# Retention plus mixture of adapters on one core: the last unit finished batch by batch, and x turned back earlier in two rounds

## The chip, the cores and the metric

The kernel runs on one core of a Trainium2 chip. The metric is the device time of one execution in microseconds. Three executions of the kernel before took 198.21, 193.67 and 198.88 us, median 198.21 us. One more execution was recorded by the profiler; it took 192.59 us.

## The reference, cut to what matters

Eight batches of eight heads, 576 positions of width 64, go through a retention (attention without softmax, with a decay for each head). Its output x, 4608 tokens of width 512, then goes through eight low-rank adapters of rank 16, of which each token uses the best two.

```python
scores = scale * q @ k.T                       # each batch and head, 576 x 576
x = (scores * Dmat) @ v                        # Dmat = gamma[h] ** (i - j) for i >= j, else 0
logits = x @ w_gate                            # 4608 x 8
w = softmax over the two largest logits
out = x + sum over those two e of w_e * (x @ A[e]) @ B[e]
```

## The kernel before, in words

**Units.** The work is cut into 18 units. Units 0 to 15 are 128 positions of a pair of batches (four chunks of positions, four pairs). Units 16 and 17 are what is left of the 576 positions: 64 positions of four batches each. Such a unit holds, on its 128 partitions, the 64 positions of one batch on the lower half and of another batch on the upper half, twice side by side; index `t` names the half and index `b` the side. Its result leaves in four stores of 64 rows (128 KB each, line 513), that of a full unit in two stores of 128 rows (256 KB each, line 508).

**Stages of a unit.** Each is a function that issues its instructions on fixed engines:

- `stage_T`/`evict_T` (`turn`): transposes k and then q on TensorE into PSUM tiles `pt_k` (banks x0, x1) and `pt_q` (banks s0, s1); ScalarE copies them out as `kT`, `qT` (lines 215, 202, 240, 235).
- `stage_U`, `stage_A`, `put_state` (`sums`, `put`): the products of k and v that carry the state from chunk to chunk (`pu`, line 300). Only full units have them; units 16 and 17 have none.
- `stage_S`, `masks` (`scores`): the scores in `ps_s` (line 269), then four masked copies by VectorE (line 289).
- `stage_X`, `evict_x` (`products`): x, transposed, in `px` (banks x0, x1, line 350); ScalarE copies it out as `xT` (line 366, for units 16 and 17 line 371).
- `stage_Z`, `routing_1` (`logits`): the products with A and w_gate in `pz` (bank x0, line 393), copied out by ScalarE as `zs` (line 406).
- `routing_2` (`choose`): VectorE finds the largest two logits (`m`, `ns`, `ge`, lines 416 to 421). `routing_3`: ScalarE's sigmoid `sg` (line 431). `routing_4`: GpSimd makes the weights `cm` (line 441) and the weighted `zc` (line 443).
- `stage_P`, `evict_z` (`small`): TensorE transposes `zc` into `pzt` (bank x1, line 378), ScalarE copies it out as `zT` (line 386).
- `stage_B` (`back`): TensorE turns x back into `po` (banks o0, o1, line 459). `stage_Y`, `evict_o` (`output`): it adds the products with B on top (line 475), and ScalarE copies the sums out as `osb`, two copies, one for each half `ho` (line 490). `store`: SyncE's queue issues the stores.

**Order.** It is written out by hand; each engine runs its instructions in the order in which the program issues them. The first rounds are listed singly. From round t = 5 on, a loop (line 726) works on several units at once: scores of unit t, logits of t - 1, `small`, `back` and `output` of t - 2, and `turn` of t + 1. Rounds 15 and 16 turn units 16 and 17, which have no state products, so no `sums` stand between `small` and `turn`. Round 17 does scores and products of the last unit, round 18 its logits and choice, round 19 what is left of it. The stores of unit t - 3 are issued at the head of round t, and those of unit 17 at the very end. All stores and nearly all loads go through SyncE's queue; one load (`Bcat`, line 588) goes through GpSimd's.

Of the kernel before, what the change touches and what calls it, by code (L numbers as in the profile page):

```python
# [10 lines left out]
FP32 = mybir.dt.float32  # L11
FP16 = mybir.dt.float16

ALU = mybir.AluOpType
AFT = mybir.ActivationFunctionType
# [3 lines left out]
def kernel(  # L19
# [10 lines left out]
    nc = tc.nc  # L30
    B, H, S, Dh = q.shape
    Ntok, Dm = out.shape
    E = moe_w_gate.shape[1]
    R = moe_A.shape[2]
    ER = E * R
    HP = H // 2
# [9 lines left out]
    scale = 1.0 / float(np.sqrt(Dh))  # L46
# [16 lines left out]
    for c in range(NFULL):  # L63
# [17 lines left out]
    mo = ctx.enter_context(tc.tile_pool(name="moe", bufs=2))  # L81
    pp = ctx.enter_context(tc.tile_pool(name="pp", bufs=1, space=bass.MemoryType.PSUM))
# [6 lines left out]
    ident16 = cpool.tile([128, 128], FP16, tag="ident16", name="ident16", align_bytes=256)  # L89
    warm = cpool.tile([128, 1], FP32, tag="warm", name="warm")  # L90
    zero = cpool.tile([128, 512], FP16, tag="zero", name="zero")
    AW = cpool.tile([128, HP, ER + E], FP32, tag="AW", name="AW", align_bytes=256)
    Bcat = cpool.tile([128, Dm], FP16, tag="Bcat", name="Bcat", align_bytes=256)
    id64 = pack[:, 0:64]
# [9 lines left out]
    units = [(c, bp) for c in range(NFULL) for bp in range(NP)] + [  # L104
        (NFULL, qd) for qd in range(NQ)
    ]
    NU = len(units)
    st = {u: {} for u in range(NU)}
# [6 lines left out]
    def is_full(u):  # L115
        return u < NU and units[u][0] < NFULL
# [18 lines left out]
    def load(u, w):  # L135
        if u >= NU:
            return
        c, bp = units[u]
        s0 = 128 * c
        if c == NFULL:  # L140
            for t in range(2):
                hf = slice(64 * t, 64 * t + 64)
                dst = block(u, t)[hf] if w == "v" else nt(u, w)[hf]
                nc.sync.dma_start(out=dst, in_=rows(w, 4 * bp + 2 * t, 2, s0, 64))
        elif w == "v":
            for t in range(2):
                hf = slice(64 * t, 64 * t + 64)
                nc.sync.dma_start(  # L148
                    out=block(u, t)[hf], in_=rows(w, 2 * bp, 2, s0 + 64 * t, 64)
                )  # L150
        elif w == "q" and paired(u):
            for b in range(2):
                nc.sync.dma_start(  # L153
                    out=nt(u, w)[64 * b : 64 * b + 64].rearrange("p (h e) d -> p h (e d)", e=2),
                    in_=q[2 * bp + b, :, s0 : s0 + 128, :].rearrange(
                        "h (p e) d -> p h (e d)", e=2
                    ),
                )
        else:
            nc.sync.dma_start(out=nt(u, w), in_=rows(w, 2 * bp, 2, s0, 128))  # L160
# [118 lines left out]
    def masks(u, b=None, order=((0, 0), (1, 0), (0, 1), (1, 1))):  # L279
        for t, ho in order:  # L280
            hf = slice(64 * t, 64 * t + 64)
            out, in0 = facing(u, t, ho)[hf], st[u]["ps"][ho][hf]
            m = (trp if paired(u) else tri)[hf].unsqueeze(1)
            if b is None:
                m = m.unsqueeze(1).broadcast_to((64, 2, HP, ST))
            else:
                out, in0 = out[:, b], in0[:, b]
                m = m.broadcast_to((64, HP, ST))
            nc.vector.tensor_tensor(out=out, in0=in0, in1=m, op=ALU.mult)  # L289
# [28 lines left out]
    def first_state(u):  # L318

        c, bp = units[u]  # L320
        if c == NFULL:
            for t in range(2):
                put_state(u, t, SP[2 * bp + t], nc.gpsimd)
        elif c > 0:
            put_state(u, 0, SP[bp], nc.gpsimd)
# [77 lines left out]
    def routing_1(u):  # L403
        s = st[u]
        zs = mo.tile([128, 2, ER + E], FP32, tag="zs", name="zs")
        nc.scalar.copy(out=zs, in_=s["pz"])  # L406
        s["zs"] = zs
# [19 lines left out]
    def routing_3(u):  # L427
        s = st[u]
        sg = mo.tile([128, 2, E], FP32, tag="sg", name="sg")
        for b in range(2):  # L430
            nc.scalar.activation(  # L431
                out=sg[:, b, :], in_=s["zs"][:, b, ER : ER + E], func=AFT.Sigmoid,
                bias=s["ns"][:, b : b + 1], scale=2.0,
            )
        s["sg"] = sg

    def routing_4(u):
        s = st[u]
        cm = mo.tile([128, 2, E], FP32, tag="cm", name="cm")
        zc = mo.tile([128, 2, ER], FP16, tag="zc", name="zc")  # L440
        nc.gpsimd.tensor_tensor(out=cm, in0=s["ge"], in1=s["sg"], op=ALU.mult)  # L441
        for b in range(2):
            nc.gpsimd.tensor_tensor(
                out=zc[:, b, :].rearrange("p (e r) -> p e r", e=E),
                in0=s["zs"][:, b, 0:ER].rearrange("p (e r) -> p e r", e=E),
                in1=cm[:, b, :].unsqueeze(2).broadcast_to((128, E, R)),
                op=ALU.mult,
            )
        s["zc"] = zc
# [20 lines left out]
    def stage_Y(u):  # L470
        s = st[u]
        bv = Bcat.rearrange("p (a o d) -> p a o d", a=HP, o=2)
        for ho in range(2):
            for b in range(2):
                nc.tensor.matmul(  # L475
                    s["po"][ho][:, b, :, :],
                    lhsT=s["zT"][:, b, :],
                    rhs=bv[:, :, ho, :],
                    start=False,
                    stop=True,  # L480
                    skip_group_check=True,
                )

    def evict_o(u):
        s = st[u]
        s["osb"] = mo.tile(
            [128, 2, HP, 2, 64], FP32, tag="osb", name="osb", bufs=3, align_bytes=256
        )
        for ho in range(2):
            nc.scalar.copy(out=s["osb"][:, :, :, ho, :], in_=s["po"][ho])  # L490

    def fill(n):
        if n == 0:
# [7 lines left out]
    o3 = out.rearrange("(b s) m -> b s m", s=S)  # L501

    def store(u):
        c, bp = units[u]
        of = st.pop(u)["osb"].rearrange("p b a o d -> p b (a o d)")
        for b in range(2):
            if c < NFULL:
                nc.sync.dma_start(
                    out=o3[2 * bp + b, 128 * c : 128 * c + 128, :], in_=of[:, b]
                )  # L510
            else:
                for t in range(2):
                    nc.sync.dma_start(
                        out=o3[4 * bp + 2 * t + b, 128 * c : 128 * c + 64, :],
                        in_=of[64 * t : 64 * t + 64, b],
                    )
# [21 lines left out]
    for dt in range(HP):  # L538
        nc.sync.dma_start(  # L539
            out=AW[:, dt, 0:ER].rearrange("p (e r) -> p e r", e=E),  # L540
            in_=moe_A[:, 128 * dt : 128 * dt + 128, :].rearrange("e d r -> d e r"),
        )
    nc.sync.dma_start(
        out=AW[:, :, ER : ER + E],
        in_=moe_w_gate.rearrange("(t p) e -> p t e", p=128),
# [9 lines left out]
    def has(u):  # L555
        return 0 <= u < NU
# [3 lines left out]
    for r in range(2):  # L560
        sl = slice(64 * r, 64 * r + 64)
# [53 lines left out]
    def ahead(t):  # L615
        for u in {4: (0,), 5: (1, 2)}.get(t, (t - 3,)):
            if t > 3 and has(u):
                store(u)
        for w in "kqv":
            load(t + 4, w)  # L620
        if has(t + 1):
            first_state(t + 1)
        if has(t + 2):
            scale_(t + 2, "k", pool2)
            scale_(t + 2, "q", pool2)

    def scores(u):
        if has(u):
            stage_S(u)
            masks(u)  # L630

    def turn(u):
        if has(u):
            for w in "kq":
                stage_T(u, w)
                evict_T(u, w)

    def back(u):
        if has(u):
            stage_B(u)  # L640

    def logits(u, tag="x0"):
        if has(u):
            stage_Z(u, tag)
            routing_1(u)

    def small(u, tag="x1"):
        if has(u):
            stage_P(u, tag)
            evict_z(u)  # L650

    def choose(u):
        if has(u):
            routing_2(u)
# [12 lines left out]
    def products(u):  # L667
        if has(u):
            stage_X(u)
            evict_x(u)  # L670

    def output(u):
        if has(u):
            stage_Y(u)
            evict_o(u)

    ahead(2)
    stage_A(2)
    logits(0)
# [43 lines left out]
    back(2)  # L723
    output(2)

    for t in range(5, NU + 2):
        if has(t - 2):
            routing_4(t - 2)
        ahead(t)
        scores(t)  # L730
        logits(t - 1)
        small(t - 2)
        choose(t - 1)
        sums(t + 1)
        if has(t - 1):
            routing_3(t - 1)
        turn(t + 1)
        back(t - 2)
        put(t + 1)
        if has(t + 1):  # L740
            shift_q(t + 1, nc.vector)
        products(t)
        output(t - 2)
    store(NU - 1)
    return


# [28 lines left out]
```

## Time and profile before

| what | before |
|---|---|
| three executions | 198.21, 193.67, 198.88 us |
| the profiled execution | 192.59 us |
| its span | 190.8 us |
| TensorE busy | 168.5 us, 88% of the span |
| ScalarE, VectorE, GpSimd busy | 114.5, 111.7, 109.2 us |
| mean granted clock of TensorE | 0.98 |

The span runs from the first to the last recorded instruction; the profiled execution's own time is 1.8 us longer. Times of rows are microseconds from the start of the span. PE is TensorE, PEld its weight loads, DVE is VectorE, ACT is ScalarE, POOL is GpSimd, SPq is SyncE's queue of DMA issues; a q behind an engine's name means its sequencer. fp32 matmuls show as two records each.

### The profile page before, as it was taken

What the parts mean: (1) busy time and instruction counts of PE and PEld (TensorE: products, weight loads), DVE (VectorE), ACT (ScalarE), POOL (GpSimd) and SP (SyncE); (2) the same over time, 40 slices, a digit from 0 to 9 for tenths busy, and PEclk for the clock granted to TensorE, in tenths of its full rate; (3) what the DMA queues carried; (4) which work ended last, traced back from release to release, by engine and by line L of the source; (5) the groups of instructions that cost most, each with busy time, mean ns of one, the idle gap of its engine ahead of it and who ended that gap; (6) DMA issues with size and microseconds to landing.
All of it is one profiled execution on the core that took longest, in us unless ns stands there. A gap on an engine that the chain in (4) does not pass through costs nothing.

```text
span 190.8 us, 10293 instructions
## 1 busy us (share of the span) xinstructions
PE 168.5 (88%) x4607; PEld 147.7 (77%) x4607; DVE 111.7 (59%) x220; ACT 114.5 (60%) x254; POOL 109.2 (57%) x161
## 2 busy tenths in 40 slices
PE   7879799858999799989999999999988999999940
PEld 2566588756888699979998898999977898889920
DVE  1593768345078286858778776768675745646000
ACT  3537081802855939576786849395867586584660
POOL 1336206459619979593958768586959396420220
PEclk9999999998799999999999999999999999999995
DMA  6999999989999999999989999999996902303245
GB/s 144 256 265 231 182 151 232 228 176 243 253 200 246 267 273 264 251 246 267 243 206 269 248 240 261 274 243 262 226 244 155 246 12 107 113 4 113 82 121 131
DMA packets 108139, 38.99 MB, mean 204 GB/s; under 512 B 88768, under 2 KB 103488, under 8 KB 108096
## 3 DMA queue, kind: packets, MB, share of 16 engines
q1 hardware_dynamic: 107952, 38.21, 81.5%
q8 instruction: 36, 0.59, 1.3%
q0 software_dynamic: 144, 0.13, 0.4%
q14 instruction: 7, 0.06, 0.1%
HBM read 29.02 MB, written 9.44 MB: 202 GB/s over the span
## 4 chain that ended last, share of the span: by engine, by line
PE 64%; SPq 17%; ACT 4%; issue 3%; DVE 3%; DMA 3%; POOL 1%; ACTq 0%; POOLq 0%; DVEq 0%
PE pz L393 16%; PE px L350 16%; PE ps_s L269 8%; PE pu L300 6%; PE pt_k L215 5%; PE po L475 5%; PE po L459 5%; SPq L153 4%; SPq L148 4%; DMA q<-in_q_dram 3%; SPq L160 3%; SPq L539 3%; PE pt_q L202 3%; SPq L521 1%; PE pzt L378 1%
## 5 line engine op out<-in xcount | busy, mean ns | idle before, releaser
L350 PE MATMUL px<-qT,v 128*64 128x64 f32 (+1 forms) x576 | 39.5, 226 | 3.5 <-issue 2.5
L179 POOL TENSOR_TENSOR k<-k,pack 128x512 f32<-128x512 f32 x32 | 35.1, 1115 | 13.1 <-DMA k<-in_k_dram 12.1
L350 PE MATMUL px<-x,v 128*64 128x64 f32 (+1 forms) x576 | 40.0, 225 | 1.2 <-issue 0.5
L350 PEld LDWEIGHTS px<-x,v 128*64 128x64 f32 (+1 forms) x576 | 36.4, 139 | 4.6 <-issue 2.0
L289 DVE TENSOR_TENSOR x<-ps_s,pack 64x512 f32<-64x512 f32 (+1 forms) x38 | 25.1, 660 | 24.1 <-PE ps_s L269 23.8
L350 PEld LDWEIGHTS px<-qT,v 128*64 128x64 f32 (+1 forms) x576 | 35.9, 139 | 3.0 <-issue 1.6
L393 PE MATMUL pz<-AW,xT 128*128 128x136 f32 x288 | 38.1, 285 | 0.1
L393 PEld LDWEIGHTS pz<-AW,xT 128*128 128x128 f32 x288 | 34.5, 190 | 2.0 <-ACT osb L490 0.7
L169 POOL TENSOR_TENSOR qs<-q,pack 128x512 f32<-128x512 f32 x27 | 27.5, 1038 | 5.5 <-DMA q<-in_q_dram 5.4
L441 POOL TENSOR_TENSOR cm<-ge,sg 128x16 f32<-128x16 f32 x18 | 4.2, 231 | 42.9 <-ACT sg L431 20.4
L406 ACT COPY zs<-pz 128x272 f32<-128x272 f32 x18 | 6.9, 386 | 35.1 <-PE pz L393 35.1
L269 PE MATMUL ps_s<-qT,kT 64*64 64x64 f32 x1152 | 23.2, 222 | 4.2 <-issue 3.5
L269 PEld LDWEIGHTS ps_s<-qT,kT 64*64 64x64 f32 x1152 | 19.7, 134 | 7.8 <-issue 5.2
L289 DVE TENSOR_TENSOR qT<-ps_s,pack 64x512 f32<-64x512 f32 (+1 forms) x38 | 25.1, 660 | 1.1
L316 POOL COPY v<-SP 64x512 f32<-64x512 f32 x32 | 20.0, 625 | 1.6
L253 DVE COPY x<-qT 64x512 f32<-64x512 f32 x17 | 15.9, 933 | 7.5 <-ACT qT L235 4.3
L490 ACT COPY osb<-po 128x512 f32<-128x512 f32 x36 | 19.2, 587 | 0.7 <-PE po L475 0.6
L366 ACT COPY xT<-px 128x512 f32<-128x512 f32 x28 | 16.4, 624 | 4.8 <-PE px L350 4.8
L300 PE MATMUL pu<-v,k 64*64 64x64 f32 x1024 | 19.2, 221 | 0.1
L240 ACT COPY kT<-pt_k 128x512 f32<-128x512 f32 x34 | 18.2, 585 | 0.9 <-PE pt_k L215 0.7
L300 PEld LDWEIGHTS pu<-v,k 64*64 64x64 f32 x1024 | 16.9, 134 | 1.7 <-DVE SP L335 0.3
L252 DVE COPY x<-qT 64x512 f32<-64x512 f32 x14 | 8.5, 607 | 15.4 <-ACT qT L235 11.4
(46 smaller groups left out, 232.4 us busy)
## 6 DMA issues: line engine op xcount, KB each, us to landing
v<-in_v_dram SPq DMA_DIRECT2D x36, 256.0 KB, 4.9
q<-in_q_dram SPq DMA_DIRECT2D x34, 256.0 KB, 5.4
out_dram<-osb SPq DMA_DIRECT2D x32, 256.0 KB, 4.3
k<-in_k_dram SPq DMA_DIRECT2D x15, 512.0 KB, 5.6
k<-in_k_dram SPq DMA_DIRECT2D x6, 256.0 KB, 4.8
out_dram<-osb SPq DMA_DIRECT2D x8, 128.0 KB, 2.4
q<-in_q_dram SPq DMA_DIRECT2D x1, 512.0 KB, 7.7
AW<-in_moe_A_dram SPq DMA_DIRECT2D x4, 64.0 KB, 3.8
```

The source lines that it names most:

```text
L169: engines[b].tensor_tensor(out=qs[:, :, 4 * b : 4 * b + 4, :].rearrange("p e h d -> p h e d"), in0=tl[:, b * H : b * H + H, :].rearrange(" ...
L179: engines[b].tensor_tensor(out=tl[:, b * H : b * H + H, :], in0=tl[:, b * H : b * H + H, :], in1=g[:, c, :].unsqueeze(2).broadcast_to((128 ...
L240: nc.scalar.copy(out=tl[:, r], in_=st[u]["p" + w][r])
L253: eng.tensor_copy(out=x2[0:64, 1, b], in_=qT[64:128, 1, b])
L269: nc.tensor.matmul(ps[ho][64 * t : 64 * t + 64, b, hp, :], lhsT=kT[sl, t, b, hp, :], rhs=qT[sl, t, b, hp, :], start=(hp == 0 and b == bs[0 ...
L289: nc.vector.tensor_tensor(out=out, in0=in0, in1=m, op=ALU.mult)
L300: nc.tensor.matmul(pu[t][64 * ho : 64 * ho + 64, b, hp, :], lhsT=kn[sl, h, :], rhs=block(u, t)[sl, h, :], start=(hp == 0 and b == 0), stop ...
L316: copy(out=dst[:, :, :, ho, :], in_=src[64 * ho : 64 * ho + 64])
L350: nc.tensor.matmul(px[b][64 * ho : 64 * ho + 64, hp, t, :], lhsT=block(u, t)[rw, b * H + 2 * hp + ho, :], rhs=facing(u, t, ho)[rw, b, hp, ...
L366: nc.scalar.copy(out=xt.rearrange("p a (t i e) -> p (a t) e i", t=2, e=2), in_=px.rearrange("p a t (e i) -> p (a t) e i", e=2),)
L393: nc.tensor.matmul(pz[:, b, :], lhsT=st[u]["xT"][b][:, dt, :], rhs=AW[:, dt, :], start=(dt == 0), stop=(dt == HP - 1), skip_group_check=True,)
L490: nc.scalar.copy(out=s["osb"][:, :, :, ho, :], in_=s["po"][ho])
```

## The change

1. In the rounds in which the unit to be turned is not a full one (rounds 15 and 16), `back(t - 2)` is issued before `turn(t + 1)` instead of after it.
2. The loop ends with round 16. The rest is written out in a new function `finish()`. In it `output` of unit 15 stands before `products` of unit 17, the stores of unit 15 directly behind, and the last unit goes through logits, choice, transposition, `back`, `output` and store for each side b by itself, in tiles of its own: `pze` in banks u0, u1, then `pzte` in the same, and `poe` in banks s0, s1 for side 0 and x0, x1 for side 1. x of the last unit is turned back into these banks in one go.
3. Of the last two units, the two copies out of PSUM for the two halves `ho` are done by ScalarE and VectorE, one each.
4. Of the stores of unit 16, those of side 0 stay on SyncE's queue and those of side 1 are issued by GpSimd. Of unit 17, three are issued by SyncE and the last by ScalarE.

```diff
-    def evict_o(u):
+    def evict_o(u, engines=(nc.scalar, nc.scalar)):
...
         for ho in range(2):
-            nc.scalar.copy(out=s["osb"][:, :, :, ho, :], in_=s["po"][ho])
+            eng = engines[ho]
+            copy = eng.copy if eng is nc.scalar else eng.tensor_copy
+            copy(out=s["osb"][:, :, :, ho, :], in_=s["po"][ho])
...
                 for t in range(2):
-                    nc.sync.dma_start(
+                    (nc.gpsimd if b and u == NU - 2 else nc.sync).dma_start(
...
+    def finish():
+        u = NU - 1
+        s = st[u]
+        store(u - 3)
+        routing_4(u - 2)
+        scores(u)
+        logits(u - 1)
+        small(u - 2)
+        back(u - 2)
+        choose(u - 1)
+        routing_3(u - 1)
+        output(u - 2)
+        routing_4(u - 1)
+        products(u)
+        store(u - 2)
+        bv = Bcat.rearrange("p (a o d) -> p a o d", a=HP, o=2)
+        pz, zs, zc, po, osb = [], [], [], [], []
+        for b in range(2):
+            pz.append(pp.tile([128, ER + E], FP32, tag=f"u{b}", name="pze"))
+            for dt in range(HP):
+                nc.tensor.matmul(
+                    pz[b], lhsT=s["xT"][b][:, dt, :], rhs=AW[:, dt, :],
+                    start=(dt == 0), stop=(dt == HP - 1), skip_group_check=True,
+                )
+        for b in range(2):
...
+            nc.scalar.copy(out=z, in_=pz[b])
+            nc.vector.max(out=m8, in_=z[:, ER : ER + E])
+            nc.vector.scalar_tensor_tensor(
+                out=ns, in0=m8[:, 0:1], scalar=-1.0, in1=m8[:, 1:2],
+                op0=ALU.mult, op1=ALU.subtract,
+            )
+            nc.vector.tensor_tensor(
+                out=ge, in0=z[:, ER : ER + E],
+                in1=m8[:, 1:2].broadcast_to((128, E)), op=ALU.is_ge,
+            )
+            nc.scalar.activation(
+                out=sg, in_=z[:, ER : ER + E], func=AFT.Sigmoid, bias=ns, scale=2.0
+            )
+            nc.gpsimd.tensor_tensor(out=cm, in0=ge, in1=sg, op=ALU.mult)
+            nc.gpsimd.tensor_tensor(
+                out=c.rearrange("p (e r) -> p e r", e=E),
+                in0=z[:, 0:ER].rearrange("p (e r) -> p e r", e=E),
+                in1=cm.unsqueeze(2).broadcast_to((128, E, R)),
+                op=ALU.mult,
+            )
+            zc.append(c)
+            if b == 0:
+                small(u - 1, "x0")
+        back(u - 1)
+        stage_Y(u - 1)
+        evict_o(u - 1, (nc.scalar, nc.vector))
+        store(u - 1)
+        def small_b(b):
+            p = pp.tile([128, 128], FP16, tag=f"u{b}", name="pzte")
+            nc.tensor.matmul(
+                p, lhsT=zc[b], rhs=ident16, is_transpose=True, start=True, stop=True
+            )
+            zt = mo.tile([128, 128], FP16, tag=f"zTe{b}", name="zTe", bufs=1)
+            nc.scalar.copy(out=zt, in_=p)
+            return zt
+        def output_b(b, zt):
+            o = mo.tile([128, HP, 2, 64], FP32, tag=f"oe{b}", name="oe", bufs=1, align_bytes=256)
+            for ho, eng in ((0, nc.scalar), (1, nc.vector)):
+                nc.tensor.matmul(
+                    po[b][ho], lhsT=zt, rhs=bv[:, :, ho, :],
+                    start=False, stop=True, skip_group_check=True,
+                )
+                (eng.copy if eng is nc.scalar else eng.tensor_copy)(
+                    out=o[:, :, ho, :], in_=po[b][ho]
+                )
...
+            for t in range(2):
+                (nc.scalar if b and t else nc.sync).dma_start(
+                    out=o3[4 * qd + 2 * t + b, 128 * c : 128 * c + 64, :],
+                    in_=of[64 * t : 64 * t + 64],
+                )
+        zt0 = small_b(0)
+        for b, tag in ((0, "s"), (1, "x")):
...
+            for dt in range(HP):
+                for ho in range(2):
+                    sl = slice(64 * ho, 64 * ho + 64)
+                    nc.tensor.matmul(
+                        po[b][ho][:, dt, :], lhsT=s["xT"][b][sl, dt, :], rhs=id64[sl, :],
+                        is_transpose=True, start=(dt == 0), stop=False, skip_group_check=True,
+                    )
+        output_b(0, zt0)
+        output_b(1, small_b(1))
...
-    for t in range(5, NU + 2):
+    for t in range(5, NU - 1):
...
-        turn(t + 1)
-        back(t - 2)
+        if is_full(t + 1):
+            turn(t + 1)
+            back(t - 2)
+        else:
+            back(t - 2)
+            turn(t + 1)
...
-    store(NU - 1)
+    finish()
     return
```

More of the change, by code (lines that the diff above doesn't have):

```diff
@@ L675, in output @@
             evict_o(u)
+    def finish():
[23 more added lines that the diff above has]
+        for b in range(2):
+            z = mo.tile([128, ER + E], FP32, tag=f"ze{b}", name="ze", bufs=1)
+            m8 = mo.tile([128, E], FP32, tag=f"m8e{b}", name="m8e", bufs=1)
+            ns = mo.tile([128, 1], FP32, tag=f"nse{b}", name="nse", bufs=1)
+            ge = mo.tile([128, E], FP32, tag=f"gee{b}", name="gee", bufs=1)
+            sg = mo.tile([128, E], FP32, tag=f"sge{b}", name="sge", bufs=1)
+            cm = mo.tile([128, E], FP32, tag=f"cme{b}", name="cme", bufs=1)
+            c = mo.tile([128, ER], FP16, tag=f"zce{b}", name="zce", bufs=1)
+            nc.scalar.copy(out=z, in_=pz[b])
[43 more added lines that the diff above has]
+                )
+            c, qd = units[u]
+            of = o.rearrange("p a o d -> p (a o d)")
+            for t in range(2):
[5 more added lines that the diff above has]
+        for b, tag in ((0, "s"), (1, "x")):
+            po.append(
+                [pp.tile([128, HP, 64], FP32, tag=f"{tag}{ho}", name="poe") for ho in range(2)]
+            )
[5 more added lines that the diff above has]
+                        is_transpose=True, start=(dt == 0), stop=False, skip_group_check=True,
+                    )
+        output_b(0, zt0)
+        output_b(1, small_b(1))
```

## The prediction

> **What bounds the kernel now.** I read the page first: busy shares and DMA issues. TensorE is busy nearly all the time; the body of the span is TensorE's, and the change leaves that work in place. The edits touch a gap in each of the two rounds that turn units 16 and 17, and the end.
>
> ```profile
> span 190.8 us, 10293 instructions
> PE 168.5 (88%) x4607; PEld 147.7 (77%) x4607; DVE 111.7 (59%) x220; ACT 114.5 (60%) x254; POOL 109.2 (57%) x161
> out_dram<-osb SPq DMA_DIRECT2D x8, 128.0 KB, 2.4
> Bcat<-in_moe_B_dram POOLq DMA_DIRECT2D x1, 128.0 KB, 5.1
> ```
>
> Second, the chain that ended last, from round 17 on (start, length, engine and line).
>
> ```profile
> 175.12 0.64 PE po L459 x16
> 175.76 2.09 PE px L350 x63
> 177.85 0.54 PE po L475 x4
> 178.39 1.87 PE pz L393 x16
> ...
> 180.34 0.39 ACT zs L406
> ...
> 181.86 0.22 POOL cm L441
> ...
> 183.20 0.64 PE po L459 x16
> ...
> 184.21 0.58 ACT osb L490
> ```
>
> The reader sees TensorE alone up to 180.26, then one chain that goes once around all engines. Third, the timelines of ScalarE and of SyncE's queue at the end.
>
> ```profile
> 175.38 0.38 ACT L386 COPY zT<-pzt 128x256 f16<-128x256 f16 x1
> 176.39 0.49 ACT L431 ACTIVATE sg<-zs,ns 128x8 f32<-128x8 f32 x2 [0.64 <-DVE ge L421]
> ...
> 181.69 1.05 ACT L490 COPY osb<-po 128x512 f32<-128x512 f32 x2
> ...
> 184.21 1.07 ACT L490 COPY osb<-po 128x512 f32<-128x512 f32 x2 [0.59 <-PE po L475]
> ```
>
> ```profile
> 182.76 5.03 SPq L513 DMA_DIRECT2D out_dram<-osb  x8
> ```
>
> Unit 16 is copied out by 182.74, and its first store is issued at 182.76. Eight issues take 5.03 us, 0.63 each. Unit 17 is copied out by 185.28, just when unit 16's four issues end (182.76 + 4 x 0.63 = 185.28). So two things end together: the chain and the row of issues. The last issue starts at about 182.76 + 5.03 - 0.60 = 187.2; with 2.4 to landing that is 189.6, and 1.2 of closing work makes the span.
>
> Fourth, the DMA engines in stretches of the end. The columns that count are the last two: busy share of the 16 DMA engines, GB/s.
>
> ```profile
> 180.30:181.80 1.50, 1.31 (x22) 0.88 (x20) 0.48 (x4) 1.17 (x5) 0.00 (x0) 1.00 0.91 350
> 182.50:183.90 1.40, 1.16 (x20) 0.88 (x21) 0.00 (x0) 0.60 (x2) 0.42 (x2) 1.00 0.00 0
> 183.90:186.60 2.70, 0.49 (x4) 0.19 (x2) 0.00 (x0) 1.07 (x2) 0.00 (x0) 0.98 0.86 200
> 186.60:189.20 2.60, 0.00 (x0) 0.00 (x0) 0.00 (x0) 0.00 (x0) 0.00 (x0) 0.50 0.84 195
> 189.20:190.80 1.60, 0.00 (x0) 0.00 (x0) 0.00 (x0) 0.00 (x0) 0.00 (x0) 0.50 0.00 0
> ```
>
> This view decides. The first stretch holds two 256 KB stores of unit 15 on 128 rows: 350 GB/s at share 0.91. The next rows hold the eight 64-row stores: the engines are as full (0.86), but move 200 GB/s. A third issue queue does not help engines that are already busy. At a full share 64-row stores would move 200 / 0.86 = 233 GB/s, so a 131072-byte store costs 0.56 us of all 16 engines, eight cost 4.5 us; they take 5.3 now (183.9 to 189.2).
>
> **Part 1: `back` before `turn` in two rounds.**
>
> ```profile
> 166.80 0.02 issue
> ...
> 166.88 0.39 ACT zs L406
> 167.27 0.04 issue
> 167.31 0.27 PE pt_k L215
> ...
> 168.30 0.51 PE pt_q L215 x16
> 168.81 0.50 PE po L459 x16
> 169.30 2.02 PE px L350 x64
> ```
>
> ```profile
> 168.17 0.49 ACT L431 ACTIVATE sg<-zs,ns 128x8 f32<-128x8 f32 x2 [0.64 <-DVE ge L421]
> 168.57 1.05 ACT L240 COPY kT<-pt_k 128x512 f32<-128x512 f32 x2
> ```
>
> TensorE stands still from 166.80 to 167.31 until `zs` frees bank x0. With `back` (0.50 to 0.64) there, the gap is filled: 0.4 to 0.5 looks won. But `back` was also the cover for the next wait. `px` needs bank x0 again, and that is free when the first `kT` copy is out: 168.57 + 0.53 = 169.10, plus about 0.1 of handover. That copy stands behind the sigmoid on ScalarE, which waits for VectorE's masks, and none of this moves. So `px` can start at 169.2 instead of 169.30: 0.1 per round, 0.2 in both (from 0 to 0.8, the gaps whole; I take the row of the `kT` copy). The rest of the 0.4 becomes a new wait of `px` for `kT`.
>
> **Part 2: round 17 and the last unit side by side.** Durations by form (last number before the idle time: mean ns of one):
>
> ```profile
> L490 ACT COPY osb<-po 128x512 f32<-128x512 f32 x10 | 5.3, 588 | 0.6 <-PE po L475 0.6
> L443 POOL TENSOR_TENSOR zc<-zs,cm 128x128 f16<-128x128 f32 x8 | 3.0, 402 | 0.3
> ...
> L371 ACT COPY xT<-px 128x512 f32<-128x512 f32 x4 | 2.4, 592 | 0.7 <-PE px L350 0.6
> ...
> L431 ACT ACTIVATE sg<-zs,ns 128x8 f32<-128x8 f32 x8 | 2.0, 293 | 2.2 <-DVE ge L421 2.2
> ...
> L406 ACT COPY zs<-pz 128x272 f32<-128x272 f32 x3 | 1.2, 386 | 5.2 <-PE pz L393 5.2
> ...
> L416 DVE MAX8 m<-zs 128x8 f32<-128x8 f32 x6 | 0.7, 161 | 4.4 <-ACT zs L406 4.4
> ...
> L417 DVE SCALAR_TENSOR_TENSOR ns<-m 128x2 f32<-128x2 f32 x3 | 0.5, 162 | 0.1
> ```
>
> ```profile
> 150.74 0.69 DVE L334 TENSOR_TENSOR sm<-pu,SP 128x512 f32<-128x512 f32 x1 [0.23 <-PE pu L300]
> ```
>
> Estimates for the new sizes, from 386 ns at 272 wide and 588 at 512 (0.84 ns a column): 0.28 for `ze` (136 wide), 0.37 for `oe` (256 wide), 0.27 for `zTe`. They can't fall under the 0.29 of an 8-wide sigmoid by much, nor exceed the full-size rows. VectorE's copies have no row of their own: 0.69 is the top (half `osb`), 0.4 my value for half of that width.
>
> On the clock of before:
>
> - `output(15)` now stands ahead of `px`; `zT(15)` is out at 175.76, as `back` ends, so no wait: L475 to 176.35, `px` to 178.4. Before, both together ended at 178.39. But ScalarE now copies `osb(15)` (1.05) ahead of `xT`: sigmoid to 176.9, `osb` to 177.85, `xT` to 178.4 and 179.05. `pze` side 0 runs 178.4 to 179.45, side 1 to 180.5; before, all ended at 180.26. A loss of 0.2.
> - Side 0: `ze` 179.8, maximum and `ns` 180.2, sigmoid 180.6, `cme` 180.9, `zce` 181.35.
> - Unit 16: `pzt` follows `pze` at 180.5; its `zT` copy stands behind side 0's `ze` and sigmoid, ends 181.1. `back` to 181.3, L475 to 181.85.
> - Side 1 queues behind that `zT`: `ze` 181.3, `ns` 181.65, sigmoid 182.05, `zce` 182.8.
> - `osb(16)`: ScalarE is free at 182.0 and copies one half to 182.55, VectorE the other beside it. Before: 182.74 for two.
> - Turning x back for both sides (0.64) ends at 182.6, beside the copies. `zTe` 182.7, products to 183.0, `oe` out at 183.5. Side 1: `pzte` 183.25, `zTe` 183.6, products 183.95, `oe` 184.45. Before: 185.28 for both.
>
> With part 1's 0.2: unit 16 is ready at 182.35 (0.4 earlier), unit 17's sides at 183.3 and 184.25 (1.0 earlier for the later). The new PSUM tiles cost nothing: u0, u1, s0, s1 have no user this late, x0 is read out as `zT(16)` by 181.1, x1 as `xT` by 179.05, before the `poe` transposes.
>
> **Part 3: stores.** Issues: SyncE has five (182.35, 183.0, 183.65, 184.3, 184.9), its last landing 2.4 later, at 187.3. ScalarE's one is issued at 184.3, behind its last copy, and lands at 186.7. GpSimd's two stand behind `zce` of side 1 (182.6).
>
> ```profile
> 16.19 0.72 POOL L588 DMA_DIRECT2D Bcat<-in_moe_B_dram  x1
> ```
>
> That one row is all there is for a DMA from GpSimd: 0.72 to issue, 5.1 to land, among many loads. So the second store lands between 183.35 + 2.4 = 185.7 (SyncE's price) and 183.35 + 5.1 = 188.4. By issues alone all is landed at 187.3.
>
> By transfers: the first packets flow 1.15 after the first issue (182.76 to 183.9 now), so at 183.5; eight stores cost 4.5 us of full engines, to 188.0; the last lands 0.4 after the packets end (189.2 to 189.6 now): 188.4. That is later than 187.3, so it sets the end. The Trainium skill, page "DMA: Bandwidth & Descriptors", section "Issuing engines are not separate DMA queues", has the same rule: DMAs from any issuer run on the same 16 engines, and several issuers save only the sequencer's time. The trace agrees with its 0.86. By the issues alone the sum would be 2.3 us, by that rule 1.2.
>
> **Sum.** Last landing 188.4 instead of 189.6: 1.2 us less. The profiled execution goes from 192.59 to 191.4, the span to 189.6. It lies 5.6 under the median of the runs shown, 198.21; the same 1.2 off that gives **197.0**, 0.6% less.
>
> **The rivals.**
> - *The halves mix.* Stores of the lower and upper 64 rows that run at the same time from different queues might reach the 350 GB/s of the 128-row stores. For it: the two kinds are equally full and differ only in rows. Against it: within SyncE's queue the two halves already alternate and stay at 200. Then issues set the end: 2.3 us, 196.0. The section "Rules for kernel authors" of the same page of the Trainium skill says that transfers to disjoint partition halves serialize; no run here shows two queues at once, so that stays open, and by it this rival falls.
> - *The transfers keep their pace.* If the engines don't get fuller than 0.86, eight stores take the same 5.3; only the head start of 0.4 remains, and less if the halved copies cost as much as whole ones: 197.8 to 198.2.
> - *GpSimd's stores decide, slower.* They are issued at about 182.6 and 183.35. If one needs over 6.2 us to land (183.35 + 6.2 = 189.6), it ends last. At twice `Bcat`'s 5.1 it lands at 193.6: 4.0 later, 202.2. For it: 5.1 is over twice the 2.4 of SyncE's. Against: `Bcat` ran among the loads, these run alone.
>
> **How the numbers follow.** Forecast 0.45, halves mix 0.22, same pace 0.23, GpSimd slower 0.10. No gain reaches 2% (4.0 us), which is about what a measurement of this kernel can tell from no change. But the three runs spread from 193.67 to 198.88, and a median of three that falls near the low run (193.67 - 1.2 = 192.5) reads as 2.9% faster: 0.25 for faster, 0.67 for within 2%, and 0.08 for slower, nearly all of it GpSimd's case. The forecast by itself lies between 196.4 and 197.8; the range goes from the low run with the gain of mixed halves (193.67 - 2.3 = 191.4) to the high run with hardly any gain (198.7).
>
> **What would show it.** Part 1: `po` L459 right behind `pzt` in rounds 15 and 16, and a gap of 0.3 to 0.4 between the end of `pt_q` and `px`. Part 2: `osb(16)` at about 182.4, the last `oe` at 184.3. Part 3: the last issue at 185, yet DMA share near 1.0 with 200 to 235 GB/s until 188. GB/s near 350 there proves the mixed halves; packets that end with GpSimd's queue prove the third rival. The prediction is wrong if unit 16's first store is issued after 182.8, or if the end moves by more than 2 us either way.

## The result, and the profile after

Over 20 executions each, the changed kernel has a median of 193.11 us (190.3 to 202.31) and the kernel before 195.37 us (192.47 to 204.18). The ratio is 0.988, with a 95% interval of 0.984 to 0.992: 1.2% faster, where 0.6% was forecast, and within the 2% that was called no change.

The profiled execution of the changed kernel is one of its slower ones (194.18 us, span 192.3), for reasons ahead of the change. So I compare distances inside an execution, from the first row of the last unit's scores (line 269 in round 17) on. Timelines of TensorE, before and after:

```profile
163.57 1.16 PE L269 MATMUL ps_s<-qT,kT 64*64 64x64 f32 x64
171.79 1.16 PE L269 MATMUL ps_s<-qT,kT 64*64 64x64 f32 x64
```

```profile
166.09 1.16 PE L269 MATMUL ps_s<-qT,kT 64*64 64x64 f32 x64
174.26 1.16 PE L269 MATMUL ps_s<-qT,kT 64*64 64x64 f32 x64
```

To the end of the span it was 190.8 - 171.8 = 19.0 us; it is now 192.3 - 174.3 = 18.0. The round before took 8.22 and takes 8.17. That is all that the trace shows of the change: 1.0 us at the end and some 0.05 in each of two rounds. All runs of the changed kernel and of the kernel before repeat it:

| run | scores of the last unit start | span | distance to the end |
|---|---|---|---|
| before | 171.79 | 190.8 | 19.0 |
| its two controls | 176.14, 178.04 | 195.1, 197.0 | 19.0, 19.0 |
| changed | 174.26 | 192.3 | 18.0 |
| its two repeats | 173.76, 175.03 | 191.8, 193.0 | 18.0, 18.0 |

ScalarE's timeline after, for the last unit; below it VectorE's. The reader finds side 0 and side 1 in turn, with unit 16's `zT` between them:

```profile
182.08 0.27 ACT L712 COPY ze<-pze 128x136 f32<-128x136 f32 x1 [0.54 <-PE pze L700]
182.84 0.30 ACT L722 ACTIVATE sge<-ze,nse 128x8 f32<-128x8 f32 x1 [0.49 <-DVE gee L718]
183.12 0.37 ACT L386 COPY zT<-pzt 128x256 f16<-128x256 f16 x1
...
184.36 0.57 ACT L492 COPY osb<-po 128x512 f32<-128x512 f32 x1
...
186.38 0.37 ACT L756 COPY oe<-poe 128x256 f32<-128x256 f32 x1 [0.38 <-PE poe L752]
187.00 0.55 ACTq L762 DMA_DIRECT2D out_dram<-oe  x1
```

```profile
184.30 0.69 DVE L492 COPY osb<-po 128x512 f32<-128x512 f32 x1 [0.16 <-PE po L475]
...
186.49 0.42 DVE L756 COPY oe<-poe 128x256 f32<-128x256 f32 x1 [0.49 <-PE poe L752]
```

Unit 16 is out at 184.99, 10.73 after the start of the scores (before 182.74, 10.95), the last side of unit 17 at 186.91, 12.65 after it (before 185.28, 13.49).

The issues of the stores after, SyncE's and GpSimd's timelines, and the page's row of what a store needs to land:

```profile
185.06 1.18 SPq L515 DMA_DIRECT2D out_dram<-osb  x2
186.34 2.23 SPq L762 DMA_DIRECT2D out_dram<-oe  x3
```

```profile
185.59 1.13 POOL L515 DMA_DIRECT2D out_dram<-osb  x2 [0.37 <-issue]
```

```profile
out_dram<-oe SPq DMA_DIRECT2D x3, 128.0 KB, 3.3
```

And the DMA engines after, in stretches of the stores (last columns: share of the engines, GB/s):

```profile
186.20:187.00 0.80, 0.26 (x2) 0.00 (x0) 0.42 (x1) 0.37 (x1) 0.52 (x1) 1.00 0.75 169
187.00:188.50 1.50, 0.00 (x0) 0.00 (x0) 0.00 (x0) 0.00 (x0) 0.00 (x0) 1.00 1.00 265
188.50:190.50 2.00, 0.00 (x0) 0.00 (x0) 0.00 (x0) 0.00 (x0) 0.00 (x0) 0.83 0.79 256
190.50:192.20 1.70, 0.00 (x0) 0.00 (x0) 0.00 (x0) 0.00 (x0) 0.00 (x0) 0.50 0.01 2
```

The stores flow for some 4.4 us instead of 5.3 and reach 265 GB/s. That is more than the 200 GB/s of before, and more than the 233 GB/s that the prediction reckoned for 64-row stores at a full share.

### The profile page after: what moved, and what is told of

It reads as the page before. It is cut to its first block, busy times and chain, and to the rows that moved or that the text cites. A ratio compares the mean times of both kernels' runs of the same rounds, so it can differ in the third digit from the quotient of the medians.

```text
span 192.3 us, 10307 instructions
## 1 busy us (share of the span) xinstructions
PE 168.5 (88%) x4607; PEld 147.8 (77%) x4607; DVE 112.5 (59%) x225; ACT 113.8 (59%) x255; POOL 109.7 (57%) x164
## 4 chain that ended last, share of the span: by engine, by line
PE 62%; SPq 15%; DVE 7%; ACT 6%; issue 4%; DMA 2%; POOL 1%; DVEq 0%; ACTq 0%
PE px L350 15%; PE pz L393 15%; PE ps_s L269 8%; PE pu L300 7%; SPq L148 5%; PE po L475 4%; PE po L459 4%; PE pt_k L215 3%; PE pt_q L202 3%; SPq L160 3%; SPq L541 3%; DMA q<-in_q_dram 2%; DVE qT L289 2%; DVE x L289 2%; SPq L153 2%
## 5 line engine op out<-in xcount | busy, mean ns | idle before, releaser
L350 PE MATMUL px<-x,v 128*64 128x64 f32 (+1 forms) x576 | 39.4, 224 | 1.6 <-ACT kT L240 0.8
L350 PEld LDWEIGHTS px<-x,v 128*64 128x64 f32 (+1 forms) x576 | 35.7, 137 | 5.7 <-issue 2.3
L393 PE MATMUL pz<-AW,xT 128*128 128x136 f32 x272 | 37.4, 292 | 0.6 <-ACT kT L240 0.6
L393 PEld LDWEIGHTS pz<-AW,xT 128*128 128x128 f32 x272 | 33.9, 196 | 3.0 <-issue 1.2
L253 DVE COPY x<-qT 64x512 f32<-64x512 f32 x17 | 14.5, 853 | 7.5 <-ACT qT L235 5.2
L240 ACT COPY kT<-pt_k 128x512 f32<-128x512 f32 x34 | 18.2, 587 | 0.8 <-PE pt_k L215 0.7
L300 PEld LDWEIGHTS pu<-v,k 64*64 64x64 f32 x1024 | 16.8, 135 | 1.7 <-DVE SP L335 0.3
L492 ACT COPY osb<-po 128x512 f32<-128x512 f32 x33 | 17.6, 585 | 0.1
L252 DVE COPY x<-qT 64x512 f32<-64x512 f32 x14 | 8.6, 615 | 15.3 <-ACT qT L235 11.3
```

Source lines behind the costliest of these rows:

```text
L240: nc.scalar.copy(out=tl[:, r], in_=st[u]["p" + w][r])
L253: eng.tensor_copy(out=x2[0:64, 1, b], in_=qT[64:128, 1, b])
L300: nc.tensor.matmul(pu[t][64 * ho : 64 * ho + 64, b, hp, :], lhsT=kn[sl, h, :], rhs=block(u, t)[sl, h, :], start=(hp == 0 and b == 0), stop ...
L350: nc.tensor.matmul(px[b][64 * ho : 64 * ho + 64, hp, t, :], lhsT=block(u, t)[rw, b * H + 2 * hp + ho, :], rhs=facing(u, t, ho)[rw, b, hp, ...
L393: nc.tensor.matmul(pz[:, b, :], lhsT=st[u]["xT"][b][:, dt, :], rhs=AW[:, dt, :], start=(dt == 0), stop=(dt == HP - 1), skip_group_check=True,)
```

## The experiments

**The changed kernel again, and a control.** The first repeat:

> The changed kernel once more, for a second profile and an interval from one chip. From the start of the last unit's scores to the end of the span it needs 117.9 us less 100, that is 17.9 us, against 18.9 before. Theory (only the end changed): again 17.9 +- 0.2, and all else differs between executions by what the first 50 us of loads take; the ratio is 0.99 to 0.995. Rival (something ahead of round 15 changed too): the stretch from 55 us to the last unit's scores is shorter by more than 0.3 us.

Ratio 0.987 (0.981 to 0.993); 18.0 us to the end. The theory holds for the end, but the ratio lies under its 0.99 to 0.995. The rival's shorter stretch is not there either: from the row of scores at 65.80 to that at 171.79 it is 106.0 us in the kernel before, from 67.35 to 173.76 here 106.4. A control, the kernel before run as if it were new:

> The kernel before, unchanged, as a control. Theory (the executions differ by what the first 50 us take, at random): ratio 1.000 with an interval of about +-0.5%, from the last unit's scores to the end 19.0 us as in the first profile. Rival (a kernel that is run as the new one reads faster by itself, and that is where the 1.2% beyond the 1.0 us of the trace come from): ratio 0.995 or less.

Ratio 1.005 (1.001 to 1.010), 19.0 us to the end. So a ratio can move by half a per cent when nothing has changed, and its interval leaves out 1.000. A third reading with a second control on the same chip:

> The changed kernel a third time, beside a second control on the same chip. Theory (the traces tell the size, 1.0 us at the end and 0.1 in the two rounds, ratio 0.9945; what the timed runs showed beyond that is scatter, as the first control's 1.0053 was): a ratio between 0.988 and 0.999, and again 18.0 us from the last unit's scores to the end. Rival (a lasting gain of some 2.4 us, of which the traces of the end hide half): 0.988 again or less.

> The kernel before as a second control, on the chip of the third reading. Theory: ratio 1.000 +- 0.005, 19.0 us from the last unit's scores to the end. If it reads 0.995 or less, the ratio of the changed kernel is to be read against it.

The changed kernel read 0.988 (0.977 to 1.000), the control 0.995 (0.991 to 0.999). Against its own control the changed kernel is 0.6% lower there, which is the 1.1 us of the trace; but by the letter of what was expected, the rival's 0.988 has come up three times.

**Part 1 alone** (`back` before `turn`, nothing else):

```diff
-        turn(t + 1)
-        back(t - 2)
+        if is_full(t + 1):
+            turn(t + 1)
+            back(t - 2)
+        else:
+            back(t - 2)
+            turn(t + 1)
```

> Part 1 alone: back before turn in the two rounds without state products, the rest as before. Theory (the filled gap comes back as a wait of px for the kT copy): the distance between the scores of successive units in these rounds goes from 8.22 to 8.17 us or 8.1, 0.05 to 0.1 each; ratio 0.999. Rival (the gap is won whole): 7.8 us per round, 0.8 in all; ratio 0.996.

Ratio 0.998 (0.993 to 1.003), 19.0 us to the end. Its timelines of TensorE and ScalarE in round 15:

```profile
163.21 0.71 PE L459 MATMUL po<-pack,xT 64*128 64x64 f32 x16
163.76 0.92 PE L215 MATMUL pt_k<-pack,k 64*128 64x64 f32 x16
164.46 0.73 PE L215 MATMUL pt_q<-pack,q 64*128 64x64 f32 x16
```

```profile
164.56 0.49 ACT L431 ACTIVATE sg<-zs,ns 128x8 f32<-128x8 f32 x2 [0.63 <-DVE ge L421]
164.95 1.05 ACT L240 COPY kT<-pt_k 128x512 f32<-128x512 f32 x2
```

`po` now fills the gap behind `pzt`. But `pt_q` ends at 165.2, and `kT`'s first copy only at 165.5, because it stands behind the sigmoid. In the changed kernel the list of waits of round 16 has that new wait by name (total, times, longest), once for the weight loads and once for the matmuls:

```profile
PEld px L350 <- ACT kT L240: 0.5, 1, 0.5
PE px L350 <- ACT kT L240: 0.4, 1, 0.4
```

Round 16 of this run takes 8.17 (168.12 to 176.30). Round 15 takes 8.52 (159.60 to 168.12); 0.36 of it is a hole inside the scores, which the profile puts down to no wait. The theory is right, at its lower end; the rival's 7.8 is not seen.

**Part 4 undone** (the changed kernel with all stores issued by SyncE):

```diff
-                    (nc.gpsimd if b and u == NU - 2 else nc.sync).dma_start(
+                    nc.sync.dma_start(
...
-                (nc.scalar if b and t else nc.sync).dma_start(
+                nc.sync.dma_start(
```

> The changed kernel, but all stores issued by SyncE (part 4 undone). Theory (SyncE's row of issues and packets of one half at a time bind the end): eight issues at 0.63 us from the first one, packets at 150 ns, 200 GB/s, last landing 7.0 us after the first issue as before; the end 0.8 to 1.2 us later than with three issuers, ratio to before about 0.998. Rival (the issuers do nothing, the gain is in the batchwise chain): the end as with three issuers, within 0.2 us, ratio 0.988.

Ratio 0.997 (0.993 to 1.001); from 176.71 to 195.5, 18.8 us. Its DMA engines:

```profile
188.70:191.30 2.60, 0.21 (x2) 0.00 (x0) 0.42 (x1) 0.37 (x1) 0.00 (x0) 0.84 0.88 203
191.30:193.90 2.60, 0.00 (x0) 0.00 (x0) 0.00 (x0) 0.00 (x0) 0.00 (x0) 0.50 0.86 200
```

200 GB/s and 5.2 us for eight stores, as before. The batchwise chain and the halved copies bring 0.2 us at the end; the other 0.8 of the 1.0 hang on who issues the stores.

**Part 4 alone** (the kernel before, with the changed issuers):

```diff
-                    nc.sync.dma_start(
+                    (
+                        nc.gpsimd if b and u == NU - 2
+                        else nc.scalar if b and t and u == NU - 1
+                        else nc.sync
+                    ).dma_start(
```

> Part 4 alone: the kernel before, with the two stores of side 1 of unit 16 issued by GpSimd and the last store of unit 17 by ScalarE; rounds, chain and copies as before. Theory (mixed halves from several queues move at up to 350 GB/s, so the stores keep up with the copies): last landing 2.4 to 3 us after the last of SyncE's three issues for unit 17 at 186.6, so 0.6 us earlier than before; from the last unit's scores to the end 18.3 us; ratio 0.996. Rival (part 4 pays only together with the batchwise chain): 18.8 to 19.0, ratio 1.0.

From 177.32 to 195.5 it is 18.2 us, as the theory had it; ratio 0.999 (0.993 to 1.005). The trace shows 0.8 us that the timed runs do not resolve (on this chip the control read the 1.005 above).

**Stores by themselves.** This kernel does nothing but stores of zeros from one tile, in five stretches with a wait between them:

```python
phase(0, [(sp, lo)] * 16)                # 64-row stores of the lower half, SyncE
phase(16, [(sp, lo), (sp, up)] * 8)      # halves in turn, SyncE
phase(32, [(sp, lo), (act, up)] * 8)     # lower by SyncE, upper by ScalarE
phase(48, [(sp, lo), (act, lo)] * 8)     # lower by both
...                                      # then four stores of 128 rows
```

> Stores alone, no other work; the output holds zeros. Four stretches of sixteen 64-row stores of 128 KB: SyncE lower half only; SyncE lower and upper half in turn; SyncE lower beside ScalarE upper; SyncE lower beside ScalarE lower; then four stores of 128 rows. Theory (the two halves of the partitions are read side by side, one half alone is slow): stretches 1, 2 and 4 at 200 to 233 GB/s, with 4 no faster than 1 in spite of two issuers, stretch 3 at 330 to 390 GB/s, so 6 us against 10 us. Rival (issue binds, halves do not matter): stretches 3 and 4 alike, both near twice stretch 1. Rival (transfers to halves serialize): stretches 3 and 4 alike, both as stretch 1.

Its windows, one in each stretch, mostly without the edges, here with the columns of VectorE, GpSimd, clock, DMA share, GB/s:

```profile
2.50:11.90 9.40, 0.00 (x0) 0.00 (x0) 1.00 0.87 203
15.10:25.40 10.30, 0.00 (x0) 0.00 (x0) 1.00 0.88 203
28.30:34.50 6.20, 0.00 (x0) 0.00 (x0) 1.00 0.94 317
37.30:47.40 10.10, 0.00 (x0) 0.00 (x0) 1.00 0.95 207
49.60:52.30 2.70, 0.00 (x0) 0.00 (x0) 1.00 0.99 382
```

A second issuer for the same half brings nothing (207 for 203). A second issuer for the other half brings half as much again (317; its sixteen stores flow for 7.1 us, those of the first, second and fourth stretch for 10.3 to 10.4). Both rivals fall, since stretches 3 and 4 are not alike. What holds back the others is seen in their issues (shortest, median and longest in ns, first and last start) and landings, first stretch 1, then stretch 4:

```profile
L41 SPq DMA_DIRECT2D out_dram<-src x16: 545/597/603, 1.4 to 11.0; - x16
...
DMA to landing us min/median/max: 2.3/2.4/2.4
```

```profile
L41 SPq DMA_DIRECT2D out_dram<-src x8: 466/884/1257, 36.2 to 42.4; - x8
...
DMA to landing us min/median/max: 2.2/4.5/5.0
```

In stretch 1 SyncE issues a store every 0.64 us, which is 205 GB/s, and each lands equally soon: nothing queues up, and the row of issues sets the pace. Stretch 2, the halves in turn, has the same issues and landings (2.2 to 2.4), so it does not tell whether one queue could move both halves side by side. In stretch 4 there are two issuers, which reach 317 GB/s in stretch 3, but the stores land up to 5.0 us after their issue and the issues themselves stretch to 1.26 us: there the one half is the limit. The two limits lie so close together that only lifting both, with two issuers and two halves, shows a gain.

**The stores dealt out by half** (the changed kernel, lower rows by SyncE, upper rows by GpSimd and, for the last store, ScalarE):

```diff
-                    (nc.gpsimd if b and u == NU - 2 else nc.sync).dma_start(
+                    (nc.gpsimd if t and u == NU - 2 else nc.sync).dma_start(
...
-                (nc.scalar if b and t else nc.sync).dma_start(
+                ((nc.gpsimd, nc.scalar)[b] if t else nc.sync).dma_start(
```

> The changed kernel, with the stores dealt out by half: the four of the lower rows by SyncE, of the upper rows three by GpSimd (unit 16's two, side 0 of unit 17) and the last by ScalarE. Theory (lower and upper rows flow side by side at 310 to 360 GB/s as in the stores alone): all packets in 3.0 to 3.4 us from 12.0 us after the last unit's scores, last landing at 15.7 instead of 16.8; to the end 16.9 us instead of 18.0, ratio 0.981 to 0.985. Rival (GpSimd's three issues of 0.55 us and its 3 us to landing bind): last landing from GpSimd's queue at 16 or later, 17.5 to 18 to the end, ratio as with the change.

From 177.49 to 195.1, 17.6 us: 0.4 less than the changed kernel, not the 1.1 of the theory. Its DMA engines:

```profile
189.50:190.20 0.70, 0.20 (x2) 0.00 (x0) 0.42 (x1) 0.37 (x1) 0.70 (x2) 1.00 0.79 179
190.20:192.00 1.80, 0.00 (x0) 0.00 (x0) 0.00 (x0) 0.00 (x0) 0.28 (x1) 0.83 0.97 298
192.00:193.70 1.70, 0.00 (x0) 0.00 (x0) 0.00 (x0) 0.00 (x0) 0.00 (x0) 0.50 0.68 224
```

298 GB/s while both halves flow, but the lower half is alone for the first 0.7 us, until GpSimd's first store, and in the last row the engines are idle for a third of the time. The ratio was 1.000 (0.995 to 1.005), so it was run again beside the changed kernel:

> The stores dealt out by half a second time, beside the changed kernel on the same chip. Theory (the end decides): 17.6 us from the last unit's scores to the end, 0.4 less than the changed kernel; ratio 0.2% under that of the changed kernel, which the timed runs may not resolve. Rival (its ratio of 1.000 was no scatter): slower than the changed kernel by 1% again.

17.6 us again (178.71 to 196.3), and a ratio of 0.989 (0.982 to 0.997) beside the changed kernel's 0.988. The same kernel has now read 1.000 and 0.989. Each divided by the control of its own chip (1.005 and 0.995), both are 0.995, where the changed kernel is 0.994: read so, the two agree, but the timed runs do not place it against the changed one. By its end it is the best version here, by 0.4 us.

**Two stores of unit 16 made one** (by half, 256 KB each):

```diff
+        if c == NFULL:
+            for t in range(2):
+                (nc.gpsimd if t else nc.sync).dma_start(
+                    out=o3[4 * bp + 2 * t : 4 * bp + 2 * t + 2, 128 * c : 128 * c + 64, :]
+                    .rearrange("b s m -> s b m"),
+                    in_=of[64 * t : 64 * t + 64],
+                )
+            return
```

> Stores by half, and unit 16's two stores of each half made one of 256 KB: two issues for unit 16 instead of four, the rest as in the stores by half. Theory (with the halves side by side the issues and GpSimd's start count next): GpSimd's two issues are over 0.5 us earlier, the last landing 15.7 to 16.4 us after the last unit's scores instead of 16.7, to the end 16.9 to 17.4. Rival (the packets set the pace whatever the number of issues): 17.5 to 17.7 as with four.

Ratio 0.992 (0.988 to 0.996); from 178.38 to 196.3, 17.9 us, 0.3 more than with four stores. A miss for the theory and for the rival: fewer issues are no gain, and GpSimd's 256 KB store takes 4.3 us to land. Why it is slower was not tried further.

**Part 3 undone** (ScalarE makes both copies of each pair):

```diff
-        evict_o(u - 1, (nc.scalar, nc.vector))
+        evict_o(u - 1)
...
-            for ho, eng in ((0, nc.scalar), (1, nc.vector)):
+            for ho, eng in ((0, nc.scalar), (1, nc.scalar)):
```

> The changed kernel with part 3 undone: ScalarE makes both copies of each pair, VectorE none. Theory (the copies stand on the chain of the last unit): unit 16's second copy puts 0.55 us ahead of zTe, and each oe pair takes 0.3 us longer, so the first store is 0.4 to 0.5 us later and the last oe 0.8 to 0.9 later; if the packets bind, the end moves by less, 0.5 us: 18.5 to 18.9 us from the last unit's scores to the end, ratio 0.992. Rival (packets hide it all): 18.0 to 18.2.

Ratio 0.997 (0.991 to 1.003); from 178.21 to 196.6, 18.4 us, 0.4 more than the changed kernel and between the theory's 18.5 and the rival's 18.2. ScalarE's queue shows the first pair as one row of 1.05 and the last store's issue 13.57 after the scores instead of 12.74:

```profile
188.31 1.05 ACT L492 COPY osb<-po 128x512 f32<-128x512 f32 x2
...
191.78 0.56 ACTq L762 DMA_DIRECT2D out_dram<-oe  x1
```

So the shared copies make the last side 0.8 us earlier, and half of that reaches the end. Part 4 alone, in the old order and with one copier, took 18.2: without the shared copies the order by sides is 0.2 us slower than the old one, and only with them 0.2 faster.

## Why the prediction was right, and where it was not

**The direction and the trace's size.** Forecast 1.2 us; the trace shows 1.1, in the places that were named. The ratio's 1.2% is twice that. Of this second half I have no place: nothing at the end or in the two rounds holds it, the instructions ahead are the same, and there the profiled executions differ by more than 6 us (scores of the last unit at 171.79 to 178.71). Two controls read 1.005 and 0.995, and the one reading that has a control on its own chip is 0.6% under it. That the rest is scatter is the likelier reading, but three readings of 0.987 to 0.988 do not show it. It stays open. The forecast time of 197.0 us is 3.9 above the measured 193.11, most of it (2.8) because the median of three executions, 198.21, was high: that of twenty is 195.37.

**Part 1: right, and small.** 0.1 per round was forecast, 0.05 measured. The reason held: the work that was moved into one gap had been the cover of the next, and `px` now waits for `kT`.

**Part 2: right to some hundredths.** Unit 16 ready 0.2 earlier on the clock of the last unit: measured 0.22 (10.95 to 10.73). Last side of unit 17 at 184.45 on the clock of before, 12.66 after the scores: measured 12.65. The estimates 0.28, 0.37 and 0.4 for the new copies came out at 0.27, 0.37 and 0.42. At the end, parts 2 and 3 together bring 0.2 us (18.8 against 19.0 with SyncE alone, 18.0 against 18.2 with three issuers); the rest of the earlier copies is lost in the stores.

**Part 3: a right sum with a wrong step.** The step that failed is "eight cost 4.5 us", from the price of 0.56 us for a store at full engines, "so it sets the end". The share of 0.86 had been read as engines that have hardly more to give. In the kernel before, though, all eight stores land equally soon after their issue (line 513):

```profile
L513 SPq DMA_DIRECT2D out_dram<-osb x8: 539/596/602, 182.8 to 187.2; - x8
...
DMA to landing us min/median/max: 2.3/2.4/2.4
```

So nothing queued up: SyncE's issues, one in 0.63 us, set the pace, and one half of the partitions would hardly have allowed more, for at the 207 GB/s of two issuers on one half a store takes 0.63 us and eight take 5.1, not 4.5. They now flow for 4.4 because the halves mix: 265 GB/s here, 317 in the stores by themselves. So a third issuer did help, and the rival of the mixed halves was right about the mechanism, at 0.22. What was held against it, that the halves in turn stay at 200 within SyncE's queue, was the pace of the issues and no evidence.

It did not bring its 2.3 us because two other terms were off the other way. The second and third of unit 17's issues by SyncE:

```profile
186.92 1.00 SPq L762 DMA_DIRECT2D out_dram<-oe  x1
188.03 0.54 SPq L762 DMA_DIRECT2D out_dram<-oe  x1
```

The second took 1.00 us instead of 0.6, so that the last one came 13.77 us after the scores instead of 13.3. And the last one landed 3.0 us after its issue, not 2.4 (the two ahead of it 3.3 and 4.0). That makes 16.8 us to the last landing, just where the sum by full engines had put it (188.4, or 188.6 without part 1's 0.2, less 171.79). Packets that are faster and issues that are later gave the same end; that the number came out so well is luck. How the 0.8 us of part 4 divides between the shorter row of issues and the mixed halves, no run here separates.

The Trainium skill, page "DMA: Bandwidth & Descriptors", section "Rules for kernel authors", says that two transfers to disjoint partition halves serialize. The prediction left that open. For two queues these runs contradict it (317 GB/s with a half each, 207 with the same half); for one queue they do not decide, since its issues alone hold it to 203.

**GpSimd's stores: no rival.** They were issued in 0.57 us each and landed after 3.0, not after `Bcat`'s 5.1 or more; among the loads at the start even `Bcat` is no measure for a quiet stretch.

**The expectations that missed.** All packets in 3.0 to 3.4 us with the stores by half (they took some 4.2) took the pace of the stores alone for the whole stretch, without the time in which only one half has a store to move. The merged stores were slower, not faster. Two missed narrowly: the 330 GB/s for two issuers on two halves (317), and the 18.5 us without the shared copies (18.4).

## What to carry to other kernels

A busy share of the DMA engines says little about their pace (0.95 stood for 207 GB/s and 0.94 for 317): read the GB/s beside it, and the times from issue to landing. Where these stay level from store to store, as the 2.3 to 2.4 us here, nothing queues up and the row of issues sets the pace; where they grow, the transfers do. Where a store covers half of the partitions, have the other half's store run at the same time from another queue: a second issuer alone gained nothing here (207 for 203 GB/s), nor did the other half alone (203). And before counting a filled gap as won, look for what the moved work had been hiding; and measure a small change by the distance between two fixed rows of the trace, which here repeats to a few hundredths of a microsecond while whole executions scatter by several.

## What the runs showed of the hardware

- 64-row stores of 2 KB rows: 203 GB/s from SyncE alone, with one half or with the halves in turn, where the issues set the pace; 207 GB/s from two issuers on one half, where the half does; 317 GB/s with a half on each of two queues; 382 GB/s as 128-row stores.
- A 64-row store takes SyncE 0.6 us to issue (5.03 for eight), against 0.33 to 0.43 for the last two 128-row stores of twice the size (unit 15's). When landings fall behind, an issue gets longer: up to 1.26 us with two issuers on one half.
- GpSimd issues such a store in 0.57 us and it lands 3.0 us later; SyncE's own land in 2.4 when no other queue runs and in 2.7 (unit 16's) and 3.3 (unit 17's) beside the other queues.
